# Later output weights, later keys, and global rows stored ahead of the last blocks: a fused attention and feed-forward kernel

## The chip, the cores and the metric

The kernel runs on one core of one Trainium2 chip. The metric is device time in microseconds (us), the median of several executions; shorter is better. PE is the matmul engine, DVE, ACT and POOL are the vector, scalar and GpSimd engines, and SP issues transfers. SP's and POOL's queues are strictly in order: a transfer waits until all that stands ahead of it on its queue has been issued.

## The reference

Sparse attention (a window of 32 positions to each side, plus 8 global positions that see and are seen by all), then a feed-forward layer with a sine activation:

```python
batch, n_heads, seq, head_dim = (8, 8, 576, 64)
scores = scale * np.matmul(q, k.transpose(0, 1, 3, 2))
mask = np.abs(pos[:, None] - pos[None, :]) <= window        # window = 32
mask = mask | is_global[:, None] | is_global[None, :]
scores = np.where(mask, scores, -1000000000.0)
...
attn = np.exp(scores); attn = attn / (np.sum(attn, axis=-1, keepdims=True) + 1e-09)
attn_out = np.matmul(attn, v)
x = attn_out.transpose(0, 2, 1, 3).reshape(B * S, H * D)    # 4608 x 512
h = x @ w_in                                                # 512 -> 2048
s = np.sin(alpha * h)
g = h + s * s / (alpha + 1e-09)
out = g @ w_out                                             # 2048 -> 512, float32
```

## The kernel before

The program is one straight list of instructions per engine, in the order in which the Python code issues them; no scheduler moves anything. It walks through the eight batches (b = 0 to 7). For each batch there is an attention and a GEMM 1 (x times w_in with the sine behind it, 16 groups of 128 columns, `gemm1`, loop over `nt`). The second product, `gemm2`, is a generator: it yields after each of its matmuls (128x512, L1172), and `fill(n)` takes n of them into PE's list wherever the code calls it. So GEMM 2 of batch b is spread over the attention and the GEMM 1 of batch b+1. How many are taken where is set by small tables: `FIRST`, `SECOND`, `NEAR`, `MIDST` in the attention (`LATE_FIRST`, `LATE_SECOND` in batch 1's), `PER_GROUP` in GEMM 1, `GROUP_LATE` in batch 1's, `GROUP_LAST` in the last one. A block of GEMM 2 is 128 rows; its 16 matmuls end in one PSUM bank (`zo`), ACT copies it to `osb` (L1182), and SP stores it (L1189). Even batches have four blocks, odd ones five.

An attention works on four head pairs (hp). For each it computes scores in two parts (PE, L929), the exponential on ACT (L938), the mask on DVE (L939), then `denominators` and, one to two pairs later, `numerators` (both PE, L967). `numerators` multiplies with V (tile VX or VD, in turn by batch) and DVE normalises with the reciprocal R into xT (L985). Batch 0 has an attention of its own.

K, Q and V come in steps. POOL casts them from DRAM to bf16 copies in DRAM (`cast_qk` L335, `cast_v` L342). SP loads V into SBUF (`load_v`, L418, four loads, the second half of them for the upper partitions) and transposes K and Q (`turn_qk`, L348) into the one pair of tiles kt and qt; DVE copies these into KX and QX (`place`, L364 and L357, eight copies per batch, the first four of them keys). `places_at` says in which attention, and behind which head pair, DVE makes which of the eight copies for the next batch. `pace(src)` is a one-element copy on POOL: as POOL's queue is in order, everything behind it waits until `src` has been written.

The weights are cast on the way from DRAM: w_in in four loads (L430), w_out in four (L436), each a quarter of the rows, 4 of the 16 `nt` steps of every block.

Global positions attend to all keys, so their rows are built from sums over all blocks (`global_sums`) and normalised at the very end. They run through the last GEMM 1 as 64 further columns (so 640 columns, not 576), and `gemm2_globals` (L1200) multiplies them with w_out and writes the 64 finished rows over the output with one indexed store on POOL (L1208), which must come after the stores of the same rows by `gemm2`. Last, `judge` tests whether the fast path's approximations hold; every engine loads the verdict (L1314) and branches (L1315) over a general path that is not run here.

The places around the change, with the counts that steer them:

```python
START = 1
FIRST, SECOND = (8, 6, 5, 5), (4, 4, 4, 4)
LATE_FIRST, LATE_SECOND = (0, 0, 3, 5), (0, 0, 3, 4)
NEAR, MIDST = 3, 6
PER_GROUP = (0, 0, 5) + 11 * (1,) + (0, 0)
```

Of the kernel before, what the change touches and what calls it, by code (L numbers as in the profile page):

```python
# [12 lines left out]
DT = mybir.dt  # L13
# [5 lines left out]
NG = 8  # L19
# [230 lines left out]
def kernel(  # L250
# [66 lines left out]
    seen = main.tile([1, 1], DT.bfloat16, name="seen")  # L317
# [21 lines left out]
    def cast_v(b):  # L339

        cast[b, "vd"] = dramp.tile([S, H, D], DT.bfloat16, name="vd")
        nc.gpsimd.dma_start(out=cast[b, "vd"][:], in_=v[b].rearrange("h s d -> s h d"))  # L342

# [553 lines left out]
    def attention(b, beside):  # L897
# [118 lines left out]
        inverse(last - 1)  # L1016
        numerators(last - 1)
        fill(NEAR)
# [87 lines left out]
    def gemm1(b):  # L1106
# [23 lines left out]
        for nt in range(NT):  # L1130
# [35 lines left out]

    def gemm2(b):
        lo, hi = (0, 4) if b % 2 == 0 else (4, 9)
        for blk in range(lo, hi):
            ops = zo[(blk + b // 2) % 2]  # L1170
            for nt in range(NT):
                nc.tensor.matmul(  # L1172
                    out=ops[:], lhsT=H2[:, nt, blk * P : (blk + 1) * P], rhs=w_out[:, nt, :],
                    start=(nt == 0), stop=(nt == NT - 1),
                )
                yield True
            osb = osbp.tile([P, DM], DT.float32, name="osb")
            if b == B - 1 and blk == hi - 1:
                for e, copy in enumerate((nc.scalar.copy, nc.vector.tensor_copy)):
                    copy(out=osb[:, e * DM // 2 : (e + 1) * DM // 2], in_=ops[:, e * DM // 2 : (e + 1) * DM // 2])  # L1180
            else:
                nc.scalar.copy(out=osb[:], in_=ops[:])  # L1182

            c = blk * P
            while c < (blk + 1) * P:
                z = min((c // QTR + 1) * QTR, (blk + 1) * P)
                run, u = c // QTR, c % QTR
                t0 = (b // 2) * 2 * S + (run // 2) * HALF + run % 2 + 2 * u
                nc.sync.dma_start(  # L1189
                    out=out[t0 : t0 + 2 * (z - c) - 1 : 2, :], in_=osb[c - blk * P : z - blk * P, :]  # L1190
                )
                c = z
# [46 lines left out]
    def pace(src):  # L1239

        nc.gpsimd.tensor_copy(out=seen[:], in_=src)  # L1241

    def phase_a(b_att, b_moe):
        def beside(at):

            if b_moe is None:
                if at == 0:
                    second_half()
                    turn_qk(1)
                    pace(turned[1][1][0:1, 0:1])  # L1250
                    load_w_in((2, 3))
                    cast_v(1)
                    load_w_out()
                    gather(v, gv)
# [28 lines left out]
    for b in range(B):  # L1283
        if b == 1:
# [30 lines left out]
    with tc.If(sure < P):  # L1315
# [31 lines left out]
```

## Time and profile before

| | us |
|---|---|
| median of 3 runs | 382.05 |
| lowest and highest run | 378.55, 384.41 |
| the profiled execution | 384.38 |
| its span, first to last instruction | 382.7 |
| PE busy | 323.6 (85%) |
| ACT busy | 288.9 (75%) |
| DVE busy | 275.5 (72%) |
| POOL busy | 55.1 (14%) |

Mean granted clock of PE: 0.97 of full speed. The profile has two kinds of rows that matter below. A timeline row gives the start in us from the span's start, the duration, the engine and source line, what it did (written tile <- read tiles) and how many instructions were merged into it; a bracket gives the engine's idle time just before and what ended it. A window row gives, for a stretch of time, its length, the busy time of PE, weight loads, DVE, ACT and POOL, the granted clock, the share of the 16 transfer engines (over 1 where transfers overlap) and the rate in GB/s. A busy PE is not PE at its peak, since matmuls overlap. "SPq" and "POOLq" are the queues' own instructions, the issue of transfers among them.

### The profile page before, as it was taken

The numbers are of one execution on the slowest core, as the hardware profiler recorded it, in microseconds if no ns is written. First come the engines' busy times: TensorE is split into PE (matmuls) and PEld (weight loads), VectorE is DVE, ScalarE is ACT, GpSimd is POOL, SyncE is SP. The second block draws the span as 40 slices with busy tenths as digits, with TensorE's granted clock in tenths as the row PEclk, the third lists the DMA queues.
The fourth block names the chain that finished last, engine by engine and source line by source line (L and its number), as shares of the span: only waits on it lengthen the run. The fifth ranks groups of instructions, "written<-read, shape, count | busy, mean of one in ns | idle before, by whom it ended". The sixth has DMA issues, their size and how long they took to land. (4 is left out here: it accounts for less than half of the span.)

```text
span 382.7 us, 10443 instructions
## 1 busy us (share of the span) xinstructions
PE 323.6 (85%) x4222; PEld 206.1 (54%) x4280; DVE 275.5 (72%) x539; ACT 288.9 (75%) x425; POOL 55.1 (14%) x78
## 2 busy tenths in 40 slices
PE   2678753699988998899899989998998998899990
PEld 2566532356645664566556655665466655554440
DVE  6966897156969687967796788778877885889400
ACT  7879794278877888879887987898888886889110
POOL 7941730014004000400030002100000000000001
PEclk9999995599999999999999999999999999999996
DMA  7999999179994991395849693977232020002221
GB/s 121 117 162 170 184 207 224 27 153 153 203 196 80 208 183 30 69 189 100 149 81 163 119 153 86 146 155 123 59 93 51 0 58 32 3 0 83 64 75 49
DMA packets 91393, 43.23 MB, mean 113 GB/s; under 512 B 76394, under 2 KB 85994, under 8 KB 90890
## 3 DMA queue, kind: packets, MB, share of 16 engines
q0 software_dynamic: 44208, 18.52, 39.9%
q1 hardware_dynamic: 47130, 23.97, 30.2%
q8 instruction: 35, 0.57, 0.6%
q14 instruction: 20, 0.16, 0.1%
HBM read 41.97 MB, written 21.95 MB: 167 GB/s over the span
## 5 line engine op out<-in xcount | busy, mean ns | idle before, releaser
L1172 PE MATMUL zo<-w_out,H 128*128 128x512 bf16 x518 | 137.5, 382 | 4.6 <-issue 3.6
L1124 PEld LDWEIGHTS <-w_in 128*128 128x128 bf16 x1024 | 99.2, 98 | 53.0 <-issue 18.7
L1172 PEld LDWEIGHTS <-H 128*128 128x128 bf16 x576 | 51.0, 98 | 45.3 <-issue 0.7
L938 ACT ACTIVATE E<-ring 128x720 bf16<-128x720 f32 x56 | 43.3, 773 | 28.8 <-PE ring L929 28.8
L1124 PE MATMUL zn<-xT,w_in 128*128 128x288 bf16 (+1 forms) x384 | 57.0, 287 | 6.1 <-DVE H L1160 4.1
L1124 PE MATMUL zr<-xT,w_in 128*128 128x288 bf16 x320 | 47.7, 287 | 3.3 <-DVE H L1160 2.9
L1124 PE MATMUL zd<-xT,w_in 128*128 128x288 bf16 x320 | 46.3, 287 | 1.9 <-DMA w_in<-in_moe_w_in_dram 1.3
L1160 DVE SCALAR_TENSOR_TENSOR H<-s,recipT,zn 128x576 bf16<-128x576 bf16 (+1 forms) x48 | 39.4, 822 | 10.7 <-ACT s L1157 7.3
L1154 ACT ACTIVATE sb<-zn,alphaT 128x576 bf16<-128x576 f32 (+1 forms) x48 | 35.7, 743 | 14.6 <-PE zn L1124 13.5
L1157 ACT ACTIVATE s<-sb 128x576 bf16<-128x576 bf16 (+1 forms) x62 | 42.7, 689 | 2.0
L1159 DVE TENSOR_TENSOR s<-sb 128x576 bf16<-128x576 bf16 (+1 forms) x66 | 30.9, 468 | 14.2 <-ACT sb L1154 13.1
L939 DVE TENSOR_TENSOR E<-E,MASKT 128x720 bf16<-128x720 bf16 x56 | 29.2, 529 | 11.6 <-ACT E L938 11.1
L1160 DVE SCALAR_TENSOR_TENSOR H<-s,recipT,zd 128x576 bf16<-128x576 bf16 (+1 forms) x40 | 32.9, 822 | 6.4 <-ACT s L1157 4.3
L1160 DVE SCALAR_TENSOR_TENSOR H<-s,recipT,zr 128x576 bf16<-128x576 bf16 (+1 forms) x40 | 32.9, 822 | 5.9 <-ACT s L1157 3.4
L1154 ACT ACTIVATE sb<-zd,alphaT 128x576 bf16<-128x576 f32 (+1 forms) x40 | 29.6, 739 | 5.9 <-PE zd L1124 5.9
L1154 ACT ACTIVATE sb<-zr,alphaT 128x576 bf16<-128x576 f32 (+1 forms) x40 | 29.6, 741 | 3.5 <-PE zr L1124 3.4
L1182 ACT COPY osb<-zo 128x512 f32<-128x512 f32 x35 | 20.4, 582 | 14.2 <-PE zo L1172 14.1
L778 ACT ACTIVATE R<-L,shift 128x576 f32<-128x576 f32 x32 | 24.8, 774 | 0.6
L985 DVE TENSOR_TENSOR xT<-zn,R 128x576 bf16<-128x576 f32 x21 | 15.8, 754 | 8.8 <-PE zn L967 6.0
L1241 POOL COPY seen<-xT 1x1 bf16<-1x1 bf16 x4 | 1.9, 480 | 134.7 <-DVE GN L755 134.7
L1208 POOL DMA_INDIRECT out_dram<-osb,grow x1 | 1.0, 979 | 135.7 <-SPq L1315 135.7
L929 PEld LDWEIGHTS <-KX 64*64 64x64 bf16 x448 | 9.0, 111 | 20.9 <-issue 19.2
(169 smaller groups left out, 373.5 us busy)
## 6 DMA issues: line engine op xcount, KB each, us to landing
kd<-in_k_dram POOLq DMA_DIRECT2D x7, 576.0 KB, 6.5
qd<-in_q_dram POOLq DMA_DIRECT2D x7, 576.0 KB, 10.1
vd<-in_v_dram POOLq DMA_DIRECT2D x7, 576.0 KB, 15.4
VX<-vd SPq DMA_DIRECT2D x16, 168.0 KB
w_in<-in_moe_w_in_dram POOLq DMA_DIRECT2D x4, 512.0 KB, 5.8
w_out<-in_moe_w_out_dram POOLq DMA_DIRECT2D x4, 512.0 KB, 16.4
out_dram<-osb SPq DMA_DIRECT2D x8, 256.0 KB
VD<-vd SPq DMA_DIRECT2D x12, 168.0 KB
```

Source lines behind the costliest of these rows:

```text
L778: nc.scalar.activation(out=R[:], in_=L[:], func=AF.Exp, scale=-1.0, bias=shift[:, 0:1])
L929: nc.tensor.matmul(out=zs[half * D : (half + 1) * D, t, 0 : G3 * WCOL].rearrange("p (m x c) -> p m x c", x=2, c=60)[:, m % G3, :, c0:c1], ...
L938: nc.scalar.activation(out=Eg, in_=zs[:, :, 0 : G3 * WCOL], func=AF.Exp, scale=scale)
L939: nc.vector.tensor_tensor(out=Eg, in0=Eg, in1=MASKT[:, None, G3 * g : G3 * (g + 1), :].rearrange("p o m c -> p o (m c)").to_broadcast([P, ...
L985: nc.vector.tensor_tensor(out=xT[:, hp, 0:S].rearrange("p (k m c) -> p k m c", k=4, c=KT), in0=tokens(nd(hp, 0)), in1=Rs[hp][:], op=ALU.mult,)
L1124: nc.tensor.matmul(out=h_part, lhsT=w_in[:, c, nt * P : (nt + 1) * P], rhs=xT[:, c, lo:hi], start=(c == 0), stop=(c == CT - 1), skip_group ...
L1154: nc.scalar.activation(out=sb[:, 0:W], in_=h, func=AF.Sin, scale=alphaT[:, nt : nt + 1])
L1157: nc.scalar.activation(out=s2[:, 0:W], in_=sb[:, 0:W], func=AF.Square)
L1159: nc.vector.tensor_tensor(out=s2[:, 0:W], in0=sb[:, 0:W], in1=sb[:, 0:W], op=ALU.mult)
L1160: nc.vector.scalar_tensor_tensor(out=H2[:, nt, r0 : r0 + W], in0=s2[:, 0:W], scalar=recipT[:, nt : nt + 1], in1=h, op0=ALU.mult, op1=ALU.add,)
L1172: nc.tensor.matmul(out=ops[:], lhsT=H2[:, nt, blk * P : (blk + 1) * P], rhs=w_out[:, nt, :], start=(nt == 0), stop=(nt == NT - 1),)
L1182: nc.scalar.copy(out=osb[:], in_=ops[:])
```

## The change

Five things change.

1. `load_w_out` moves from batch 0's attention to batch 0's GEMM 1 (nt = 10), behind the copies of the global keys and queries, and a `pace` on one column of VX[1]'s upper half stands ahead of it. On POOL's queue it is now ahead of the casts of batch 2's K and Q.
2. For batch 3, `places_at` gives the first two key copies behind head pair 2 and the other six behind the attention, where it gave 2, 1, 3 and 2 at four places.
3. In every attention but batch 0's, `fill(NEAR)` stands ahead of `numerators(last - 1)` and not behind it.
4. The global rows are multiplied and stored ahead of the last batch's five blocks. So that these blocks do not write other values over batch 7's global rows, POOL first copies batch 7's eight global columns of H2 onto their token columns (`put_globals`). The columns' numbers are worked out on DVE and loaded into POOL registers ahead of batch 2's GEMM 1 (`load_columns`). `GROUP_LAST` takes 16 matmuls of GEMM 2 into the last GEMM 1 instead of 4, and the rest of batch 6's stands ahead of the global rows.
5. The last block is computed in two halves of 256 columns, in two PSUM banks, each evicted by ACT and stored by itself (`store`). The closing branch has its preferred side changed.

```diff
@@ numerators and fill
         inverse(last - 1)
+        fill(NEAR)
         numerators(last - 1)
-        fill(NEAR)
         denominators(last)
@@ gemm1, b == 0 and nt == 10
                 load_vg(1)
+                pace(VX[1][D : D + KT, 0, 0, 0:1])
+                load_w_out()
@@
+    def load_columns():
+        ...
+        nc.vector.tensor_copy(out=ci[:, 0], in_=gi32[:, 0::2])
+        ...
+        nc.vector.tensor_scalar(out=gcol[:], in0=cf[:, 3], scalar1=float(S), scalar2=None, op0=ALU.add)
+        for j in range(NG):
+            columns_of.append(nc.gpsimd.value_load(gcol[0:1, j : j + 1], min_val=S, max_val=2 * S - 1))
+
+    def put_globals():
+        for j, c in enumerate(columns_of):
+            g = 2 * S + j * B + B - 1
+            nc.gpsimd.tensor_copy(out=H2[:, :, bass.ds(c, 1)], in_=H2[:, :, g : g + 1])
@@ gemm2
+            parts = 2 if (b, blk) == (B - 1, hi - 1) else 1
+            for part in range(parts):
+                cols = slice(part * DM // parts, (part + 1) * DM // parts)
+                if part:
+                    ops = zd[:, 1]
+                for nt in range(NT):
+                    nc.tensor.matmul(
+                        out=ops[:, cols], lhsT=H2[:, nt, blk * P : (blk + 1) * P], rhs=w_out[:, nt, cols],
+                        start=(nt == 0), stop=(nt == NT - 1), skip_group_check=True,
+                    )
+                    yield True
+                nc.scalar.copy(out=osb[:, cols], in_=ops[:, cols])
+                store(b, blk, osb, cols)
@@
-    GROUP_LAST = (0, 0, 2) + 2 * (0, 0, 0, 1) + 5 * (0,)
+    GROUP_LAST = (0, 0, 3) + 13 * (1,)
@@ places_at
-        share = {-1: (0, 2), 1: (2, 3), 2: (3, 6), 4: (6, 8)}
+        share = {2: (0, 2), 4: (2, 8)} if b_att == 2 else {-1: (0, 2), 1: (2, 3), 2: (3, 6), 4: (6, 8)}
@@ phase_a, batch 0
                     cast_v(1)
-                    load_w_out()
                     gather(v, gv)
@@ main loop and tail
     for b in range(B):
+        if b == 2:
+            load_columns()
...
-    waiting.append(gemm2(B - 1))
+    put_globals()
     square_x(B - 1, 0)
     square_x(B - 1, 1)
-    for c in range(CT):
+    square_w(0)
+    fill(NT)
+    square_w(1)
+    fill(4 * NT)
+    gemm2_globals()
+    judge_sums()
+    waiting.append(gemm2(B - 1))
+    for c in (2, 3):
         square_w(c)
         fill(NT)
-        if c == 1:
-            judge_sums()
     judge()
     fill(2 * NT * NT)
-    gemm2_globals()
...
-    with tc.If(sure < P):
+    with tc.If(sure < P, preferred_fallthrough_block=False):
```

How the instructions move is seen in each engine's list. First POOL's, from w_in's second half to the copy that releases batch 2's V (`vd`, `kd`, `qd` are the DRAM copies, `seen` the target of `pace`). Before:

```order
L430 DMA w_in<-in_moe_w_in_dram 128x4x512 x2
L342 DMA vd<-in_v_dram 4608x1x64
L436 DMA w_out<-in_moe_w_out_dram 128x4x512 x4
L1260 COPY MASKT<-MASK 64x720 x2
L719 CAST VGb<-H_97 64x512
L377 COPY KX_94<-kTg 128x48x8
L380 COPY QX_96<-qTg 128x4x7x4 x2
L335 DMA kd<-in_k_dram 32x9216
L335 DMA qd<-in_q_dram 32x9216
L1241 COPY seen<-qt 1x1
```

And in the changed kernel:

```order
L435 DMA w_in<-in_moe_w_in_dram 128x4x512 x2
L343 DMA vd<-in_v_dram 4608x1x64
L1294 COPY MASKT<-MASK 64x720 x2
L724 CAST VGb<-H_97 64x512
L382 COPY KX_94<-kTg 128x48x8
L385 COPY QX_96<-qTg 128x4x7x4 x2
L347 COPY seen<-VX_93 48x1
L441 DMA w_out<-in_moe_w_out_dram 128x4x512 x4
L336 DMA kd<-in_k_dram 32x9216
L336 DMA qd<-in_q_dram 32x9216
L347 COPY seen<-qt 1x1
```

The four loads of w_out have moved behind the four other POOL copies and a copy that reads VX, and stand directly ahead of batch 2's K and Q.

Next DVE's list at the end of batch 2's attention, from the last global sums to the first group of GEMM 1 (`kt`, `qt` are batch 3's transposed keys and queries). Before:

```order
L755 TENSOR_REDUCE GN<-zd 128x2x4
L357 COPY QX_96<-qt 64x4x6x48 x2
L1159 TENSOR_TENSOR s_2256<-sb 128x576
L1160 SCALAR_TENSOR_TENSOR H_97<-s_2256,recipT,zn 128x576
L1160 SCALAR_TENSOR_TENSOR H_97<-s_2263,recipT,zr 128x576
```

And in the changed kernel:

```order
L760 TENSOR_REDUCE GN<-zd 128x2x4
L369 COPY KX_94<-kt 64x48x24 x2
L362 COPY QX_96<-qt 64x4x6x48 x4
L1180 COPY ci<-girow 1x8
L1181 TENSOR_SCALAR ci<-ci 1x8
L1182 CAST cf<-ci 1x16
L1183 TENSOR_SCALAR cf<-cf 1x8
L1186 SCALAR_TENSOR_TENSOR cf<-cf 1x8
L1189 SCALAR_TENSOR_TENSOR cf<-cf 1x8
L1192 TENSOR_SCALAR gcol<-cf 1x8
L1166 TENSOR_TENSOR s_2340<-sb 128x576
L1167 SCALAR_TENSOR_TENSOR H_97<-s_2340,recipT,zn 128x576
```

Four more copies and seven one-row instructions now stand between the attention and the first group's square; the two key copies that stood ahead of the attention's first masks are gone from there.

Last, SP's list at the end of the program (the stores of the last blocks, the verdict and the branch). Before:

```order
L1314 TENSOR_LOAD verdict
L1314 ISA x2
L1189 DMA out_dram<-osb 80x512
L1189 DMA out_dram<-osb 48x512
L1189 DMA out_dram<-osb 96x512
L1189 DMA out_dram<-osb 32x512
L1189 DMA out_dram<-osb 112x512
L1189 DMA out_dram<-osb 16x512
L1189 DMA out_dram<-osb 128x512
L1315 COMPARE_AND_BRANCH
```

And in the changed kernel:

```order
L1228 DMA out_dram<-osb 96x512
L1228 DMA out_dram<-osb 32x512
L1354 TENSOR_LOAD verdict
L1354 ISA x2
L1228 DMA out_dram<-osb 112x512
L1228 DMA out_dram<-osb 16x512
L1228 DMA out_dram<-osb 128x256 x2
L1355 COMPARE_AND_BRANCH
L1355 UNCONDITIONAL_BRANCH
```

The verdict is loaded two blocks later, the last block's store has become two, and an unconditional jump follows the compare. POOL's indexed store is no longer behind these stores: the first store of the last batch waits for it. PE's list has, behind the last GEMM 1, 39 matmuls of batch 6's GEMM 2 where 50 stood, then the 32 of the global rows, then batch 7's blocks.

More of the change, by code (lines that the diff above doesn't have):

```diff
@@ L316 @@
     VG0 = main.tile([NG * B, D], DT.bfloat16, name="VG0")
-    seen = main.tile([1, 1], DT.bfloat16, name="seen")
+    seen = main.tile([P, 1], DT.bfloat16, name="seen")
+    gcol = main.tile([1, NG], DT.int32, name="gcol")
     girow = main.tile([1, NG], DT.int64, name="girow")
@@ L342, in cast_v, with pace @@
         nc.gpsimd.dma_start(out=cast[b, "vd"][:], in_=v[b].rearrange("h s d -> s h d"))
+    def pace(src):
+        nc.gpsimd.tensor_copy(out=seen[0 : src.shape[0]], in_=src)
     def turn_qk(b):
```

46 lines of the change are left out of this document (24 added, 22 removed).

## The prediction

> **What bounds the kernel now.** I read the page first (busy shares, slices, granted clock), then the waits of PE, then the timeline stage by stage. The page's last three slices rows say where to look: the granted clock is full except around 57 to 77 us, and the transfer engines stand still in the slice that follows their fullest one.
>
> ```profile
> PEclk9999995599999999999999999999999999999996
> DMA  7999999179994991395849693977232020002221
> ```
>
> From batch 2 on PE is the bound: matmuls follow each other with gaps of tenths. Three places are not so: attention 1, attention 2 and the end. The largest is the first, where PE waits twice for V; these are PE's rows (start, duration, what; in brackets the idle time before and its end):
>
> ```profile
> 67.89 0.28 PE L967 MATMUL zn<-E,VX 56*64 56x88 bf16 x2 [4.82 <-DMA VX<-VGb]
> 70.56 0.78 PE L967 MATMUL zn<-E,VX 56*64 56x88 bf16 x26 [2.39 <-DMA VX<-VGb]
> ...
> 78.01 0.82 PE L1172 MATMUL zo<-w_out,H 128*128 128x512 bf16 x3
> ```
>
> 4.82 + 2.39 = 7.2 us are lost there, and the work could have started at 67.89 - 4.82 = 63.1. Why V is late is seen in POOL's and SP's own queues: w_out is issued right behind batch 1's V cast, V's four loads into SBUF leave SP only when that cast has landed, and then w_out and the next batch's K and Q (52.22) are on the same engines.
>
> ```profile
> 38.41 2.26 POOL L342 DMA_DIRECT2D vd<-in_v_dram  x1
> 40.12 3.53 POOL L436 DMA_DIRECT2D w_out<-in_moe_w_out_dram  x4
> ...
> 52.22 0.53 POOL L335 DMA_DIRECT2D kd<-in_k_dram  x1
> ...
> 83.97 0.18 POOL L1241 COPY seen<-qt 1x1 bf16<-1x1 bf16 x1 [30.65 <-DMA qt<-qd]
> ```
> ```profile
> 51.60 1.63 SPq L418 DMA_DIRECT2D VX<-vd  x4
> ...
> 75.18 2.21 SPq L348 DMA_TRANSPOSE kt<-kd  x1
> ...
> 93.61 1.60 SPq L418 DMA_DIRECT2D VD<-vd  x4
> ```
>
> **V and w_out (term A).** w_out leaves the queue ahead of batch 1's loads and comes back behind a copy that waits for V's second half. V's cast landed by 51.60, and this is kept: w_out stood behind it in the same queue. What V's loads take on engines that do nothing else is shown by batch 7, whose loads are issued at 282.59; the columns that matter are the last two, DMA share and GB/s:
>
> ```profile
> 282.59 1.68 SPq L418 DMA_DIRECT2D VX<-vd  x4
> ```
> ```profile
> 52.00:54.00 2.00, 1.22 (x10) 0.68 (x7) 1.89 (x5) 1.92 (x3) 1.32 (x3) 1.00 1.24 208
> 62.00:64.00 2.00, 0.69 (x14) 0.33 (x14) 1.95 (x6) 0.87 (x2) 0.00 (x0) 0.50 1.28 273
> 288.00:290.00 2.00, 2.00 (x17) 1.53 (x16) 1.33 (x2) 1.97 (x3) 0.00 (x0) 1.00 0.28 45
> 290.00:292.00 2.00, 1.76 (x13) 1.11 (x12) 1.31 (x3) 1.97 (x4) 0.00 (x0) 1.00 0.00 0
> ```
>
> All is moved by 290.0, 7.4 us after the first issue, against 70.56 - 51.60 = 19.0 in batch 1. So V lands at the latest at 51.60 + 7.4 = 59.0, ahead of 63.1: the V wait goes. What is late next is w_out, the first thing PE needs behind V.
>
> ```profile
> w_in<-in_moe_w_in_dram POOLq DMA_DIRECT2D x4, 512.0 KB, 5.8
> w_out<-in_moe_w_out_dram POOLq DMA_DIRECT2D x4, 512.0 KB, 16.4
> ```
>
> The nearest row for an undisturbed 512 KB load is w_in's, 5.8 us. With half a microsecond for the copy, the first quarter lands at 59.0 + 0.5 + 5.8 = 65.3, each further one 524 KB at 208 GB/s = 2.5 us later (the window from 52, when mostly w_out moved): the fourth at 72.9. PE takes w_out in fills of 3, 3, 5 and 4 matmuls; the thirteenth, the first that needs the fourth quarter, is the second of the fill at 78.01, so at 78.2, or at 71.0 with 7.2 us gone. It would stand 1.9 us there: A = -5.3. If V's second half, which is what the copy waits for, lands 2 us ahead of the last of the six loads, nothing is waited for: A = -7.2. I take **-6.0**; with w_out's row of 16.4 it would be far less (a rival). PE's half clock (0.50 in the window from 62) moves along with the stage.
>
> Behind w_out on POOL stand batch 2's K and Q. They land about 73 + 2 x 2.5 = 78, but today SP comes to their transposes only at 75.18, held by the late attention. So the copy of qt that releases the next casts stays near 83.97, and V of batch 2 near 93.61 + 7.4 = 101. Its reader comes at 115.11, or 109: this hides it.
>
> ```profile
> 115.11 0.48 PE L967 MATMUL zn<-E,VD 56*64 56x88 bf16 x28
> ```
>
> **Batch 3's keys (term B).** DVE stands 3.29 us for their transpose, ahead of the masks of attention 2. The table loads mark the stages: attention 2 lasts 126.05 - 107.00 = 19.05, attention 4, without such a wait, 204.51 - 187.17 = 17.34. The change gains the 1.7 between.
>
> ```profile
> 107.00 1.28 ACT L905 ACT_TABLE_LOAD   x1
> 126.05 1.28 ACT L1021 ACT_TABLE_LOAD   x1
> 187.17 1.28 ACT L905 ACT_TABLE_LOAD   x1
> 204.51 1.28 ACT L1021 ACT_TABLE_LOAD   x1
> ```
> ```profile
> 111.68 0.92 DVE L364 COPY KX<-kt 64x1152 bf16<-64x1152 bf16 x2 [3.29 <-DMA kt<-kd]
> ...
> 127.42 0.93 DVE L357 COPY QX<-qt 64x1152 bf16<-64x1152 bf16 x2
> 128.97 0.46 DVE L1159 TENSOR_TENSOR s<-sb 128x576 bf16<-128x576 bf16 x1 [0.62 <-ACT sb L1154]
> ...
> 359.11 0.15 DVE L1095 TENSOR_SCALAR oks<-cm 128x1 f32<-128x1 f32 x1
> ```
>
> But behind the last normalisation DVE now does six copies instead of two (4 x 0.46 = 1.8) and seven one-row instructions for the column numbers (at 0.15, 1.1), with the first square of GEMM 1 queued behind them: 2.9 us, less the 0.62 that DVE idles there now, is 2.3. PE gets its fourth group's PSUM that much later; I take 2.0, since a little of PE's idle time there is used. B = **+0.3**, from -1.7 (pile hidden) to +2.3 (no gain in the attention). The eight register loads on POOL wait for this too; only the cast for batch 5, which waits for a later attention anyway, is behind them.
>
> **Three fills ahead of the numerators (term C).** In seven attentions PE now goes from one run of fills to the products and no longer turns to 128-row weights between numerators and the last denominators. Such a turn costs what PE idles at it:
>
> ```profile
> 201.94 0.59 PE L1172 MATMUL zo<-w_out,H 128*128 128x512 bf16 x2 [0.16 <-issue]
> ```
>
> 7 x 0.16 = **-1.1**; a second turn saved would double it to -2.2. The numerators now end three fills later, 3 x 0.22 = 0.66, and DVE's normalisation reads them; but it waits for the reciprocal from ACT there, 2.6 us in six attentions:
>
> ```profile
> DVE xT L985 <- ACT R L778: 2.6, 6, 0.9
> ```
>
> So 0.43 of each 0.66 is covered, and the rest would be 7 x 0.23 = +1.6, if anything waited for it: that is the upper end.
>
> **The last GEMM 1 and the tail (term D).** The order has 39 matmuls of batch 6's GEMM 2 behind the last GEMM 1, where 50 stood: 11 move in.
>
> ```profile
> 326.82 1.25 PE L1124 MATMUL zn<-xT,w_in 128*128 128x288 bf16 x8 [0.60 <-DVE H L1160]
> 327.90 1.25 PE L1124 MATMUL zr<-xT,w_in 128*128 128x288 bf16 x8
> ...
> 332.02 1.25 PE L1124 MATMUL zr<-xT,w_in 128*128 128x288 bf16 x8
> ...
> 342.12 1.25 PE L1124 MATMUL zn<-xT,w_in 128*128 128x288 bf16 x8
> 343.21 13.98 PE L1172 MATMUL zo<-w_out,H 128*128 128x512 bf16 x62
> ```
>
> One matmul is 13.98 / 64 = 0.22 (two records are missing). Out of the tail go 11 x 0.22 = 2.4. A group is 1.08 of PE (326.82 to 327.90) but comes every (342.12 - 332.02) / 8 = 1.26, so 0.18 of each fill is free and 0.04 is not: 0.5 in all if all of it fits, 2.4 if none does; I take 0.9. The last block in halves has 32 matmuls of 256 columns; at the group's pace, 1.08 / 8 = 0.135 for about 320, each takes some 0.12 with its weights, 3.8 instead of 16 x 0.22 = 3.5. D = -2.4 + 0.9 + 0.4 = **-1.1**, from -2.0 to +0.4. The eight column copies on POOL lie beside the 39 fills and the global rows (39 x 0.22 + 1.9 = 10.5 us).
>
> **The end (term E).** Behind PE's last matmul, 372.06 + 1.94 = 374.0, come 8.7 us today: evictions, the last store's landing at 375.7 (issued 373.07), then the scatter, its landing near 381, and the closing barriers, 1.7.
>
> ```profile
> 372.06 1.94 PE L1200 MATMUL zd<-w_out,H 128*64 128x256 bf16 x32
> ```
> ```profile
> L1208 POOLq EVENT_SEMAPHORE  x5: 17/43/43, 368.3 to 375.7; - x5
> ```
> ```profile
> L1342 SPq EVENT_SEMAPHORE  x14: 17/28/28, 381.0 to 382.6; - x14
> ```
> ```profile
> L1315 PEldq COMPARE_BRANCH  x1: 4318/4318/4318, 373.2 to 373.2; - x1
> ```
>
> With the scatter ahead of the last stores the end is one half's eviction (0.5), a landing (2.6) and 1.7: 4.9. The scatter itself is hidden by five blocks of 3.5 us. But PE's branch, 4.3 us from 0.8 before its last matmul's end, was covered by the scatter and is so no longer: 3.5 + 0.1 + 1.7 = 5.3. The branch's preferred side changes, which may or may not remove that; I take 5.3, so E = **-3.4**, at best -3.8. [...]
>
> **Rivals.** *w_out comes as slowly as now.* Its row of 16.4 from the fourth issue at 59.5 + 2.2 gives 78.1, as late as it is used today: A = 0, and the rest, -5.3, remains: 376.8. For it: K and Q of batch 2 still follow it. Against: 208 GB/s needs no 16 us.
>
> *The two transfers in a row, slower than before.* They are now side by side. If each keeps its duration, V lands at 67.89 and the fourth quarter at 68.4 + 2.2 + 16.4 = 87.0, against 78.2 in use: A = +8.8, total +3.5: 385.6. This mechanism decides from a landing of 78.2 + 5.3 = 83.5 on. Against it stands the engines' full share beside V (1.28 from 62), so that they do slow each other.
>
> [...]
>
> **How the numbers follow.** -6.0 + 0.3 - 1.1 - 1.1 - 3.4 = -11.3. The profiled execution took 384.38 (span 382.7, and 1.7 around it) and would take 373.1; it lies 2.3 above the median of 382.05, whose own runs spread over 5.9, so the forecast is 382.05 - 11.3 = **370.8**, its own range 366 to 375. Chances: forecast 0.62, slow w_out 0.18, late copies 0.12, transfers in a row 0.04, anything worse 0.04. A range of 366 to 378 takes in the first three but for their outer ends. A change of 2%, 7.6 us, is about what a measurement of this kernel tells: faster means under 374.4. Nine tenths of the forecast and half of the late copies lie there, and a little of slow w_out: 0.63. Slower (over 389.7): 0.05. The rest, 0.32, is no change.
>
> **What would show it.** In the changed profile: no wait for V in batch 1's attention, w_out's loads landing in 6 to 9 us and a PE wait of 0 to 2 us at L1214 ahead of the fourth fill; attention 2 near 17.3 us with GEMM 1 of batch 2 some 2 us longer; PE's fills each about 0.22 between the last groups; the scatter landed while blocks are still computed, and 5 us from the last matmul to the end. It is wrong if w_out's median landing stays at 16, if the casts behind qt move later than 84, or if PE waits for POOL at the tail.

## The result, and the profile after

The changed kernel takes 377.26 us (18 runs, 374.88 to 379.64), the kernel before 381.1 (18 runs, 378.27 to 387.73). The ratio is 0.991, with a 95% interval of 0.988 to 0.994: shorter by 0.9%, which is clear of the noise but under the 2% that the prediction set for a change, and not the 3% forecast. Ratios, here and below, are against executions of the kernel before on the same chip, and leave out those more than 1.5% above the fastest of their kernel. The profiled execution of after has a span of 377.93, against 382.68; both are longer executions than their medians, so the 4.75 us between them is not quite the 3.84 between the medians.

The table loads mark the stages, as in the prediction (ACT loads one table at the start of each attention and one at the start of each GEMM 1). With PE's last matmul they divide the 4.75 us between the two spans:

| stage | before | after | difference |
|---|---|---|---|
| up to attention 1 | 54.87 | 55.67 | +0.80 |
| attention 1 | 27.33 | 22.22 | -5.11 |
| GEMM 1 of batch 1 | 24.80 | 24.80 | 0 |
| attention 2 | 19.05 | 20.80 | +1.75 |
| GEMM 1 of batch 2 | 21.72 | 24.25 | +2.53 |
| attention 3 to attention 7 | 173.24 | 172.15 | -1.09 |
| last GEMM 1 up to the last matmul | 52.98 | 51.53 | -1.45 |
| from there to the end | 8.69 | 6.51 | -2.18 |

The first two rows belong together. Over all profiles of this document attention 1 starts anywhere from 54.9 to 58.7, but ends at 77.3 to 78.4 where w_out's move is in and at 81.5 to 83.2 where it is not: the move's gain up to there is -5.11 + 0.80 = -4.3 here.

In attention 1 the waits went nearly as forecast. PE's rows there, and POOL's that set them:

```profile
65.06 0.58 PE L1214 MATMUL zo<-w_out,H 128*128 128x512 bf16 x1 [0.15 <-DMA w_out<-in_moe_w_out_dram]
...
68.66 0.59 PE L1214 MATMUL zo<-w_out,H 128*128 128x512 bf16 x2 [0.60 <-DMA w_out<-in_moe_w_out_dram]
...
71.20 0.81 PE L1214 MATMUL zo<-w_out,H 128*128 128x512 bf16 x3 [0.82 <-DMA w_out<-in_moe_w_out_dram]
...
73.77 1.46 PE L1214 MATMUL zo<-w_out,H 128*128 128x512 bf16 x5 [0.83 <-DMA w_out<-in_moe_w_out_dram]
```
```profile
58.56 0.19 POOL L347 COPY seen<-VX 48x1 bf16<-48x1 bf16 x1 [5.90 <-DMA VX<-vd]
59.02 3.01 POOL L441 DMA_DIRECT2D w_out<-in_moe_w_out_dram  x4 [0.27 <-issue]
...
84.97 0.18 POOL L347 COPY seen<-qt 1x1 bf16<-1x1 bf16 x1 [21.75 <-DMA qt<-qd]
```

V is there at 58.5, no matmul waits for it, and the four waits for w_out come to 2.4 us. But the last row is where it was: the copy that releases the next casts stood at 83.97 before and stands at 84.97 now. By the start of attention 3 (147.77 before, 147.74 after) the whole gain is gone. These are ACT's marks of attention 2, GEMM 1 of batch 2 and attention 3, and PE's rows in between:

```profile
102.69 1.28 ACT L910 ACT_TABLE_LOAD   x1
123.49 1.28 ACT L1026 ACT_TABLE_LOAD   x1
147.74 1.28 ACT L910 ACT_TABLE_LOAD   x1
```
```profile
111.29 0.28 PE L972 MATMUL zd<-E,ones 56*64 56x88 bf16 x8
114.26 0.41 PE L972 MATMUL zd<-E,ones 56*64 56x120 bf16 x20 [2.69 <-issue]
114.60 1.04 PE L1214 MATMUL zo<-w_out,H 128*128 128x512 bf16 x4
...
116.94 1.91 PE L1214 MATMUL zo<-w_out,H 128*128 128x512 bf16 x4 [0.34 <-issue]
...
130.37 1.14 PE L1129 MATMUL zn<-xT,w_in 128*128 128x288 bf16 x8 [2.47 <-DVE H L1167]
```

There are two holes. In the first PE stops in the middle of a set of 28 denominator matmuls, behind the eighth, and waits for nothing that the profile shows. Soon after, four matmuls of a fill take 1.91 us instead of 1.04. The windows (columns as in the prediction) show why: the granted clock, the third column from the end, falls to a half.

```profile
112.00:114.00 2.00, 0.00 (x0) 0.00 (x0) 1.07 (x3) 0.29 (x1) 1.37 (x3) 1.00 1.15 77
114.00:116.00 2.00, 1.74 (x49) 1.05 (x52) 0.59 (x2) 0.65 (x1) 1.86 (x2) 0.92 1.47 315
116.00:118.00 2.00, 1.67 (x34) 1.06 (x26) 1.96 (x4) 1.82 (x3) 0.43 (x1) 0.50 1.03 194
```

The second hole, 2.47 us, is the pile on DVE ahead of the first groups of GEMM 1:

```profile
124.87 0.93 DVE L369 COPY KX<-kt 64x1152 bf16<-64x1152 bf16 x2
125.82 1.86 DVE L362 COPY QX<-qt 64x1152 bf16<-64x1152 bf16 x4
127.72 0.16 DVE L1180 COPY ci<-girow 1x8 int32<-1x8 int32 x1
...
128.95 0.44 DVE L1166 TENSOR_TENSOR s<-sb 128x576 bf16<-128x576 bf16 x1
```

At the end, the last matmul is over at 369.51 + 1.91 = 371.42. PE's branch, now a compare and a jump, is in the second block (its two parts, shortest, median and longest in ns, and their starts):

```profile
369.51 1.91 PE L1214 MATMUL zd<-w_out,H 128*128 128x256 bf16 x16
```
```profile
L1355 PEldq COMPARE_BRANCH  x2: 91/2030/3970, 370.3 to 371.6; - x2
```

### The profile page after: what moved, and what is told of

Same layout as the page of the kernel before. It is cut to its first block, busy times and chain, and to the rows that moved or that the text cites. A ratio compares the mean times of both kernels' runs of the same rounds, so it can differ in the third digit from the quotient of the medians.

```text
span 377.9 us, 10527 instructions
## 1 busy us (share of the span) xinstructions
PE 323.3 (86%) x4238; PEld 208.2 (55%) x4296; DVE 277.5 (73%) x545; ACT 288.7 (76%) x426; POOL 59.6 (16%) x87
## 4 chain that ended last, share of the span: by engine, by line
PE 45%; DMA 15%; DVE 14%; ACT 13%; issue 6%; POOL 5%; SPq 0%; DVEq 0%; ACTq 0%; POOLq 0%
PE zo L1214 22%; PE zn L1129 8%; ACT sb L1161 6%; DVE H L1167 5%; PE zr L1129 4%; DMA kt<-kd 4%; PE zd L1129 4%; DMA vd<-in_v_dram 3%; DMA w_out<-in_moe_w_out_dram 3%; PE ring L934 2%; DVE s L1166 2%; DMA kd<-in_k_dram 2%; PE zn L972 2%; DMA VD<-in_v_dram 2%; PE zd L972 2%
## 5 line engine op out<-in xcount | busy, mean ns | idle before, releaser
L1214 PE MATMUL zo<-w_out,H 128*128 128x512 bf16 (+1 forms) x518 | 137.5, 380 | 7.2 <-issue 3.9
L1214 PEld LDWEIGHTS <-H 128*128 128x128 bf16 x592 | 53.2, 98 | 47.8 <-issue 4.6
L1219 ACT COPY osb<-zo 128x512 f32<-128x512 f32 (+1 forms) x36 | 20.7, 574 | 13.9 <-PE zo L1214 7.7
L1201 POOL COPY H<-H 128x16 bf16 x8 | 5.0, 629 | 105.4 <-DVE H L1167 104.9
```

Source lines behind the costliest of these rows:

```text
L1214: nc.tensor.matmul(out=ops[:, cols], lhsT=H2[:, nt, blk * P : (blk + 1) * P], rhs=w_out[:, nt, cols], start=(nt == 0), stop=(nt == NT - 1) ...
L1219: nc.scalar.copy(out=osb[:, cols], in_=ops[:, cols])
```

## The experiments

The first question was what ate the gain of attention 1. One theory (K) said that batch 3's keys come at a fixed time; a rival (S) that PE's stall and the pile are troubles of their own.

**w_out's move alone**, in the kernel before:

```diff
                 load_vg(1)
+                pace(VX[1][D : D + KT, 0, 0, 0:1])
+                load_w_out()
...
                     cast_v(1)
-                    load_w_out()
```

> The kernel before with w_out's move alone. Theory K (the keys of batch 3 land at a fixed time, because their cast waits for batch 2's queries, so that an earlier attention 2 only waits longer for them): attention 1 lasts 22.2 us as in the changed kernel instead of 27.3, and DVE's wait for kt in attention 2 grows from 3.3 to 7 or 8 us, attention 2 from 19.05 to 23 or 24. The time is 0 to 1 us below the kernel before. Rival S (the keys move along with the earlier work, and what the changed kernel lost in attention 2 came from PE's stall there and from the pile of copies): the wait for kt stays at 3 us, attention 2 at 19, and the time is 4 to 5 us below the kernel before.

387.72 us, *longer* than the kernel before: ratio 1.019 (1.012 to 1.027). Attention 1 lasts 22.20, as in the changed kernel, but attention 2 27.94 instead of 19.05. DVE's and PE's rows, and two windows:

```profile
113.18 0.92 DVE L368 COPY KX<-kt 64x1152 bf16<-64x1152 bf16 x2 [9.16 <-DMA kt<-kd]
```
```profile
114.72 0.96 PE L971 MATMUL zd<-E,ones 56*64 56x88 bf16 x28 [6.68 <-DVE E L943]
```
```profile
112.00:113.00 1.00, 0.00 (x0) 0.00 (x0) 0.00 (x0) 0.00 (x0) 0.00 (x0) 0.50 0.20 38
...
118.00:119.00 1.00, 1.00 (x30) 0.67 (x21) 0.93 (x3) 1.00 (x2) 0.00 (x0) 0.50 0.00 0
```

K holds in that the keys do not come earlier, and both theories missed a second loss. The keys land at 113.18 (111.68 before), though attention 2 starts 4.4 us earlier; DVE waits 9.16 for them instead of 3.29, and in and behind that wait PE runs at half clock, from 111 to 121.

**The late keys undone**, the rest of the change kept:

```diff
-        share = {2: (0, 2), 4: (2, 8)} if b_att == 2 else {-1: (0, 2), 1: (2, 3), 2: (3, 6), 4: (6, 8)}
+        share = {-1: (0, 2), 1: (2, 3), 2: (3, 6), 4: (6, 8)}
```

> The changed kernel with batch 3's copies at their four old places. Theory K: DVE waits 7 to 8 us for kt at the start of attention 2, attention 2 lasts 23 to 24 us (20.8 in the changed kernel), GEMM 1 of batch 2, with the seven one-row instructions but without the four more copies, 22.8 (24.25): together 46 to 47 against 45.05, and the time is 0 to 2 us above the changed kernel. Rival S: attention 2 19 and GEMM 1 22.8, together 41.8, and the time 3 us below the changed kernel: the late placing is then a loss.

382.09 us, 4.8 above the changed kernel, ratio to before 1.004 (1.000 to 1.009). Attention 2 takes 27.32 (DVE waits 10.26 for kt, PE 7.78, half clock again), GEMM 1 of batch 2 22.37. So without the late placing nothing is left of w_out's gain, and the seven one-row instructions alone cost 0.65 of GEMM 1.

**The clock's share.** w_out's move alone again, with 28 further matmuls of 128x512, whose result is not used, where PE waits for the keys:

```diff
+            if b == 2 and hp == 1:
+                warm(zd[:, 0], 28)
             if hp:
                 denominators(hp - 1)
```

> The kernel before with w_out's move alone, and 28 further matmuls of 128x512 (6.1 us at full clock; their result is not used) where PE waits 6.7 us for batch 3's keys in attention 2. It computes the same besides. Theory H (of the 8.9 us that attention 2 lost there, 4.4 are the longer wait for the keys, and the other 4 to 5 are PE's half clock from 111 to 121, which follows the idle time): the granted clock stays at 1.00 through attention 2, which falls from 27.9 to 23.0 to 24.0, and the time is 4 to 5 us below w_out's move alone, about that of the kernel before. Rival (the clock does not matter, since DVE and the transfers bound that stage): attention 2 stays at 27 to 28.

```profile
112.00:114.00 2.00, 2.00 (x11) 0.91 (x10) 0.00 (x0) 0.00 (x0) 0.00 (x0) 1.00 1.14 73
```

The clock stays at 1.00 throughout, attention 2 falls from 27.94 to 25.59, and the time from 387.72 (386.30 to 389.21) to 385.31 (382.60 to 387.34). So the half clock is some 2.4 of the 8.9 us, not the 4 to 5 expected; the rest is the wait. DVE's copy comes 11.2 us after the start of attention 2 (114.23 - 103.01), where it was 4.7 before the change: 6.5 later, not 4.4, and 19.05 + 6.5 = 25.6. (In w_out's move alone the copy came 10.55 after the start; by the same sum its wait explains 5.9 and the half clock 3.0.) The keys did not only stand still. SP issues their transpose at 103.44 before and 103.43 with w_out's move alone, but they land 1.5 us later; why was not tested.

**No pile, no copies in attention 2.** The changed kernel with batch 3's copies one by one in the groups of GEMM 1, and the column numbers in attention 1:

```diff
+            if b == 2 and 4 <= nt < 12:
+                which, t, y = PLACES[nt - 4]
+                place(b + 1, which, t, y, nc.vector.tensor_copy)
...
+            if b_att == 1 and at == 2:
+                load_columns()
```

> The changed kernel without the pile: batch 3's eight copies go one by one into groups 4 to 11 of GEMM 1 of batch 2 (group 11's square moves from DVE to ACT), and the column numbers are worked out in attention 1, where DVE idles. If the pile is what GEMM 1 of batch 2 lost: it falls from 24.25 to 21.7 to 22.5 us, and attention 2, without any copy, from 20.8 to 17.3 if PE's stall of 2.7 us does not recur, or to 19 to 20 if it does. The time is 2 to 5 us below the changed kernel. Rival (GEMM 1 of batch 2 is held by something else, or DVE has no room for eight copies between its groups): GEMM 1 of batch 2 stays above 23.5 and the time within 1 us of the changed kernel.

377.23 us, as the changed kernel: the rival was right. Attention 2 is 20.31 with the same stall (2.43 us, again behind the eighth of 28 matmuls, at full clock after it, and a second one of 1.15), and GEMM 1 of batch 2 is 23.89: PE waits about half a microsecond for DVE at one group after another. DVE has no room for eight copies there, whether in a pile or apart.

**Earlier casts.** The copy that holds back the casts of batch 2's V and batch 3's K and Q reads kt instead of qt:

```diff
-            pace(turned[2][0][0:1, 0:1])
+            pace(turned[2][1][0:1, 0:1])
```

> The changed kernel with one edit: the copy that holds back the casts of batch 2's V and batch 3's K and Q reads kt, which is written first, and not qt. The casts are issued at 81 to 82 us instead of 86.3, so batch 3's transposes leave SP at about 99 to 100 instead of 103.3. Theory F (PE's stall of 2.7 us in attention 2 is a load of its instructions that runs while qt's transposes are moved, and the half clock follows from it): qt has been moved by 112, the stall shrinks below 1 us, the clock stays full, and attention 2 falls from 20.8 to 17.3 to 18.5; the time is 2 to 4 us below the changed kernel. Rival (the stall belongs to the place in PE's list, or casts and transposes beside each other slow one another by as much): a stall of 2 us and more stays, and the time is within 1 us of the changed kernel.

374.95 us, ratio to before 0.988 (0.978 to 0.998), 2.3 below the changed kernel; the interval takes in the changed kernel's 0.991, so that the stages have to tell. The casts came only 1.7 us earlier (from 84.53, not 86.26) and the keys' transpose 1.3 (102.04, not 103.31). That was enough for attention 2, which is 17.22. PE's rows there and at the pile, and a window behind the pile:

```profile
112.45 0.41 PE L972 MATMUL zd<-E,ones 56*64 56x120 bf16 x20 [0.68 <-issue]
...
127.00 1.59 PE L1129 MATMUL zn<-xT,w_in 128*128 128x288 bf16 x8 [2.46 <-DVE H L1167]
```
```profile
128.00:130.00 2.00, 2.00 (x9) 1.12 (x8) 0.86 (x2) 1.34 (x3) 0.00 (x0) 0.50 1.07 163
```

The stall shrank with the transposes, as theory F said. The pile is now the first long stop of PE, and this time the half clock follows *it*: GEMM 1 of batch 2 is 25.33 instead of 24.25.

What PE waits for in the stall is seen only in the trace's transfer records, where the engines' own instructions come in as 16 KB transfers (queue q8, 35 of them in the changed kernel). The table sets the first of these after attention 2's start beside SP's issue of the queries' transpose (which stands behind the keys'):

| kernel | attention 2 starts | queries' transpose issued by | load starts | PE stands |
|---|---|---|---|---|
| earlier casts, spread copies, old w_out (below) | 107.31 | 108.22 | 111.96 | 0 |
| before | 107.00 | 111.62 | 113.05 | 0 |
| changed | 102.69 | 113.77 | 111.63 | 2.69, to 114.26 |
| changed, copies in GEMM 1 | 102.29 | 113.28 | 111.13 | 2.43, to 113.59 |
| earlier casts | 102.91 | 111.94 | 109.80 | 0.68, to 112.45 |
| earlier casts, spread copies | 102.12 | 110.98 | 108.84 | 0.36, to 111.36 |

SP is done with the queries' transpose when the keys have landed, within 0.1 us (111.62 and 111.68 in the kernel before). Where the transposes are long issued, the load starts 4.65 us after attention 2, when PE has begun some 2,000 of its instructions. Where they are not, it starts 2.11 to 2.16 us before SP is done with the second one, in all eleven profiles of that kind (at PE's instruction 2,231 in the changed kernel), and where PE stands it goes on 2.4 to 2.65 us after the load's start. It comes to that spot 8.9 us after attention 2's start in each of them. So the load waits among the keys' transposes, and PE can stand for it. That the stall follows the transposes was tested; that the transfer is PE's is read from a count: 33 of these transfers start ahead of the last matmul, one for some 260 of PE's 8,583 instructions, and no other engine has more than 738.

**The pile undone as well.** On top of the earlier casts, three copies behind head pair 2, three behind head pair 3 and two at the end of attention 2, and the column numbers in attention 1:

```diff
-        share = {2: (0, 2), 4: (2, 8)} if b_att == 2 else {-1: (0, 2), 1: (2, 3), 2: (3, 6), 4: (6, 8)}
+        share = {2: (0, 3), 3: (3, 6), 4: (6, 8)} if b_att == 2 else {-1: (0, 2), 1: (2, 3), 2: (3, 6), 4: (6, 8)}
```

> The edit of the run before, and batch 3's eight copies spread over attention 2 (three behind head pair 2, three behind head pair 3, two at the end), and the column numbers worked out in attention 1. Theory (GEMM 1 of batch 2 is longer by what DVE has to do at its head: 1.9 us for four more copies, 0.6 for the one-row instructions): GEMM 1 of batch 2 goes back from 24.25 to 21.7 to 22.3, attention 2 is 0.5 to 1 us longer than without the spread, together 1 to 2 us less than with the earlier casts alone and 3 to 6 us below the changed kernel. Rival (DVE's work is the bound of attention 2 and GEMM 1 together, wherever the copies stand, as eight copies inside GEMM 1 made it 23.9): the two together do not get shorter.

```profile
102.12 1.28 ACT L910 ACT_TABLE_LOAD   x1
119.03 1.28 ACT L1026 ACT_TABLE_LOAD   x1
140.76 1.28 ACT L910 ACT_TABLE_LOAD   x1
```

372.31 us, ratio 0.983 (0.976 to 0.989). Attention 2 is 16.91 and GEMM 1 of batch 2 21.73: both losses are gone, and the copies cost nothing there. Together the two stages are 2.4 us shorter than even the prediction expected of the change itself (17.3 and 2 us more than 21.72).

**The end.** The kernel before with parts 4 and 5 alone, which is the changed kernel without parts 1 to 3 (w_out and the key copies as in the two edits at their old places, and the fills):

```diff
         inverse(last - 1)
-        fill(NEAR)
         numerators(last - 1)
+        fill(NEAR)
```

> The kernel before with the global rows, the column copies, the halves and the branch alone (parts 4 and 5). From the two traces: 1.4 us less between the last GEMM 1 and the last matmul, 2.2 less behind it, and up to 1.1 more at the head of GEMM 1 of batch 2 for the seven one-row instructions: 2.5 to 3.6 us below the kernel before. By the terms of the prediction (1.1 and 3.4) it would be 4.5. Rival (the end moves with each run, and the traces only happened to differ): within 1 us of the kernel before, with 8 us or more from the last matmul to the end.

379.92 us, against 381.84 for the kernel before beside it (four executions between 373.86 and 381.65, too far apart for a verdict). The stages are clear: 51.54 up to the last matmul and 6.66 behind it, as in the changed kernel (51.53 and 6.51), against 52.98 and 8.69; GEMM 1 of batch 2, with the one-row instructions, is 22.34, 0.6 longer. The differences at the end belong to these parts. Next, the changed kernel with the old branch:

```diff
-    with tc.If(sure < P, preferred_fallthrough_block=False):
+    with tc.If(sure < P):
```

> The changed kernel with the closing branch as before, everything else kept. If the preferred side bought nothing, as the prediction took it: the same 6.5 us from the last matmul to the end, with PE's branch at 4.0 to 4.3 us. If it is worth something: up to 1 us more here. Rival: the branch without the jump behind it falls through without a stall, PE's branch is under 0.2 us, and the end comes no earlier than the last store's landing allows, about 5.5 to 6.5 us.

```profile
L1355 PEldq COMPARE_BRANCH  x1: 3742/3742/3742, 371.7 to 371.7; - x1
```

None of the three expectations held. There is still a stall, 3.74 us, but the end comes 4.71 us after the last matmul instead of 6.51. The single branch starts at 371.7, 1.1 *before* the last matmul's end at 372.77. In the changed kernel the compare is quick (91 ns), and the jump behind it stalls for 3.97 from 371.62, 0.2 *after* the last matmul's end at 371.42. But it is not PE that the end waits for. These are SP's waits for its stores to land (L1355), and SP's and PE's arrivals at the closing barrier (L1382), first in the changed kernel and then in this run:

```profile
L1355 SPq EVENT_SEMAPHORE  x8: 17/17/17, 372.4 to 375.3; - x8
L1382 SPq DRAIN  x3: 7/7/13, 376.7 to 377.3; - x3
L1382 PEldq DRAIN  x2: 8/40/73, 375.6 to 377.4; - x2
```
```profile
L1355 SPq EVENT_SEMAPHORE  x8: 17/17/17, 374.1 to 375.1; - x8
L1382 SPq DRAIN  x3: 7/7/13, 375.9 to 376.4; - x3
L1382 PEldq DRAIN  x2: 8/8/8, 375.6 to 376.5; - x2
```

In the changed kernel PE is at the barrier at 375.6, and SP, behind the last landing at 375.3 and a jump of its own, at 376.7.

In both kernels SP issues the last store 0.4 us after the last matmul, but it lands 3.9 us after the matmul with the jump and 2.3 without. The transfer records show the difference. With the jump, a 16 KB instruction load runs from 1.1 to 2.7 us after the last matmul, beside the store, and 9 of the store's 144 packets end only behind it, at 2.8 to 3.4. Without the jump the load is over at 1.1, and all packets have ended by 1.8. So it is in all seven profiles that have the jump (landing at 3.7 to 4.1) and in the five that have the old branch and the halves (2.2 to 2.8). The new preferred side costs 1.8 us; that it does so mainly by a load in the store's way is read from these records and was not tested by itself.

The whole time, 376.28 (374.00 to 379.27), is 1.0 below the changed kernel's, but its ratio to the kernel before, 0.991, is the same, so the time by itself proves nothing.

**Earlier casts, spread copies and the old branch together**, the three edits shown:

> The earlier casts, the spread copies and the early column numbers, with the closing branch as before the change (no jump behind the compare). From the two runs that did the one and the other: 1.6 to 1.8 us from the last matmul to the end less than with the jump (4.7 for 6.35), attention 2 and GEMM 1 of batch 2 at 16.9 and 21.7 us, 370 to 371 us in all, 10 to 12 below the kernel before. Rival (the jump's 1.8 us was a difference between two runs): the end stays at 6.3 to 6.7 and the time at 372 to 373.

370.72 us, ratio 0.974 (0.970 to 0.979), with 4.89 us behind the last matmul: the fastest version, 6.5 us below the changed kernel. And with the last block whole:

```diff
-            parts = 2 if (b, blk) == (B - 1, hi - 1) else 1
+            parts = 1
```

> The same kernel with the last block computed and stored whole. By the prediction's terms its 16 matmuls take 3.5 us and 32 halves 3.8, and a whole eviction 0.6 and a half 0.4: the last matmul comes 0.2 to 0.4 us earlier and the time behind it is 0.2 to 0.3 longer where the store's landing bounds the end, and not longer where PE's branch does. So the time stays within 0.5 us. Rival (the halves are what shortens the end): 1 us and more longer behind the last matmul.

371.70 us, and 5.79 behind the last matmul: a microsecond longer, so the rival's reading holds for the end. PE's branch is over before the last matmul ends here; what is later is the last store's landing, 3.6 us after the last matmul where it was 2.2. The halves themselves cost nothing ahead of it (51.58 with the whole block, 51.53 without), not the 0.4 of the prediction. (Attention 2 happened to start 0.9 earlier in this profile, at 102.09, and was 1.5 longer, 18.37: PE stood 1.46 us in the same stall, until 112.42. With the transposes where they are, coming earlier is no gain.)

**What is w_out's move worth?** In the changed kernel:

```diff
                 load_vg(1)
-                pace(VX[1][D : D + KT, 0, 0, 0:1])
-                load_w_out()
...
                     cast_v(1)
+                    load_w_out()
```

> The changed kernel with w_out loaded at its old place, everything else kept. Theory (the move of w_out saved 5 us in attention 1 and lost most of it again in attention 2, since PE came too early for its own instructions): attention 1 lasts 26 to 27.5 us (22.2 in the changed kernel), attention 2, with the late key copies and no stall, 17.0 to 17.6 (20.8), GEMM 1 of batch 2 still 24 (the pile stays): 1 to 2 us above the changed kernel. Rival (the move is worth its 5 us): 5 us above it, at 382. Other rival (V's wait is short in most executions and only the profiled one showed it long): at or below the changed kernel.

The load at its old place gives 379.01 us (377.95 to 380.31), 1.7 above the changed kernel; but the kernel before was slower beside these runs too (385.16), and the ratio, 0.985 (0.981 to 0.989), is no worse than the changed kernel's 0.991. In the profile, attention 1 is 25.42, attention 2 16.35 without any stall, GEMM 1 of batch 2 25.20 with the half clock behind the pile: 66.97 together, against 22.22 + 20.80 + 24.25 = 67.27. The move gains 3.2 in the first stage and gives it back in the other two together. In the kernel with the earlier casts, the spread copies and the old branch, the same edit:

> The kernel of the run before, with w_out loaded where the kernel before loads it. If the move of w_out is worth its whole 5 to 6 us as soon as the keys of batch 3 are no longer waited for: attention 1 lasts 27 us instead of 21.4, attention 2 and GEMM 1 of batch 2 stay at 17 and 21.7, and the time is 4.5 to 6 us above the run before. Rival (something behind attention 1 is set by transfers and takes the gain back here too): the time is within 2 us of it.

372.94 us, but between 367.91 and 376.07: no answer. Both were therefore timed again, side by side:

> The kernel with the earlier casts, the spread copies and the old branch, with w_out at its old place, in more executions than before, since four of them lay between 367.9 and 376.1. If the move of w_out is worth 4 to 5 us there: a median 4 to 5 above the same kernel with the move, 374.5 to 375.5. If V's wait varies from one execution to the next and is short in about half of them: a median 0 to 2.5 above it, with a spread of 8 us against 2.4.

> The same kernel with w_out's move, on the same chip as its counterpart: 370 to 371.5, with a spread of 2 to 3 us.

374.19 us (373.03 to 375.47) without the move, 371.02 (369.94 to 372.14) with it: 3.2 us, ratios to before 0.972 and 0.964. The spread expected of the former, 8 us, did not come; V's wait was long again:

```profile
70.45 1.11 PE L972 MATMUL zn<-E,VX 56*64 56x88 bf16 x28 [6.60 <-DMA VX<-VGb]
```

So the move is worth 3.2 us once attention 2 can take it, close to nothing in the kernel as changed (by the ratios it may even cost a little), and costs 6 alone. The two executions near 368 to 370 of the first attempt stay unexplained.

## Why the prediction was wrong, by its own steps

| term | predicted | in the traces |
|---|---|---|
| V and w_out (A) | -6.0 | -5.1, in attention 1 |
| batch 3's keys (B) | +0.3 | +4.3 |
| fills ahead of the numerators (C) | -1.1 | -1.1, in attentions 3 to 7 |
| last GEMM 1 and tail (D) | -1.1 | -1.45 |
| the end (E) | -3.4 | -2.2 |
| start of the program | 0 | +0.8 |
| sum | -11.3 | -4.75 |

**A's mechanism was right in itself, and failed at what comes behind it.** V landed by 58.5 (59.0 was the bound), w_out took 9.8 us at the median (6 to 9 were said), PE waited 2.4 (0 to 2). The computed -5.3 was closer than the -6.0 chosen, and -4.3 is what is left at the end of attention 1. The step that failed is "So the copy of qt that releases the next casts stays near 83.97 ... this hides it". The first half came nearly true (84.97, where the prediction had named later than 84 as a sign of being wrong) and should have been the alarm: attention 2 came 4.3 us earlier (102.69, not 107.00), and behind that copy stand not only batch 2's V, whose reader I looked up, but batch 3's keys as well, and their transposes. I priced the keys in B from the kernel before, where attention 2 starts at 107, and added the two terms. They do not add: A without the late placing is +6 in the runs, A with it about 0.

**B.** "The change gains the 1.7 between": without w_out's move attention 2 gains more, 2.7 (19.05 to 16.35, some 0.4 of it from C, as in the attentions behind it). With it, the stall of 2.69 and the half clock behind it stand in its place, and attention 2 is 1.75 longer. Of the pile "I take 2.0": PE's hole was 2.47 and GEMM 1 grew by 2.53, and by 3.5 to 3.6 where the half clock followed. The order of DVE's list had been read rightly; the clock had no term. Whether it follows a stop is partly luck, as the last section shows.

**C and D have the right sum, C by luck.** The -1.1 of C is the sum over attentions 3 to 7: the 3rd, 5th and 6th are 0.4 shorter each, the 7th 0.2, and the 4th 0.35 longer, for a reason that stays open (over the profiles with the moved fills it lasts 17.0 to 17.7, with the old ones 17.3 to 18.1). So where the fills gain, they gain more than the 0.16 per attention of the prediction, nearer to the doubled figure that it named; some 0.4 more stands in B's row. In D the 0.4 for the halves was not there; without it the prediction's terms give -1.5, and -1.45 was measured. The column copies on POOL took 5.46 us, 0.68 each, and lay beside the fills, and PE waited for none of them; no run shows a hold-up that would bear out the 0.12 given to late copies. The slow w_out and the transfers in a row did not come either.

**E named the wrong last wait, at "PE's branch, 4.3 us from 0.8 before its last matmul's end".** The stall's length was about right (3.97), but the jump stalls after the last matmul and not before it. Even so PE is not the last at the closing barrier. The end goes by the path that the prediction gave for its best case, with other sizes: 0.4 to the last store's issue, 3.4 for its landing (2.6 had been taken) and 2.6 behind it (1.7 had been taken), together 6.5. With the old branch it is 0.4 + 1.9 + 2.4 = 4.7, so that the best case of 4.9 comes out with sizes that make up for each other. That PE's stall would stay was an estimate from the 4.32 us of the kernel before. It held: the stall is 3.97 and 3.79 on the jump (the changed kernel; earlier casts and spread copies) and 3.74 and 3.56 on the single compare (the old branch; the same with these casts and copies). I did not see that an instruction load would run beside the last store, from 1.1 to 2.7 us behind the last matmul.

None of the rivals' mechanisms was at work. The time came out where the slow w_out would have put it (376.8), for another reason.

## What to carry to other kernels

When a stage is pulled forward, list everything further on that keeps its own time (transfers behind a pacing copy, the transposes behind these, the engines' own instruction loads), not only the next reader; a term priced at the old start of the stage cannot be added to the gain. A stop of PE of some 2.5 us at the head of GEMM 1 of batch 2 cost another microsecond in the clock (3.5 to 3.6 us in all) or nothing (2.53), by where it lay in the clock's steps. The end came 6.51 us after the last matmul where the closing branch's stall began behind that matmul and an instruction load ran beside the last store, and 4.71 where the stall began 1.1 us ahead of that matmul's end: in a kernel like this one the branch is best placed so that both come under the last matmuls.

## What the runs showed of the hardware

- With transposes in flight a load of instructions (PE's, by the count above) came up to 4.3 us later here (8.9 instead of 4.65 us after attention 2's start), and PE stood up to 2.69 us for it. In the five profiles in which the load came with the transposes done or nearly so, PE did not stand for it.
- The granted clock changed in steps: in the kernel before and the changed kernel all stretches at half clock, but for the one at the program's end, last 3.41 us or a whole multiple of it (17.07; 10.24 and 3.41), and so do the stretches at full clock that follow them (300.37; 47.79 and 256.00). In attention 2 and GEMM 1 of batch 2 it fell to a half behind stops of 2.20, 2.46 and 2.69 us, for 3.41 us each, and did not fall behind stops of 1.46, 2.43 and 2.47. Where a fall shows how the steps lie, 2.0 us of the stop of 2.69, 2.1 to 2.5 of the stops of 2.46 and the whole one of 2.20 lay inside the step ahead of the fall, while the stop of 2.47, which no fall followed, was cut into 1.43 and 1.04. How the stop of 2.43 lay is not shown, nor a bound that holds elsewhere: in attention 1 of the changed kernel the clock, at a half already, stayed there from 64.48 to 67.89 behind a step in which PE stopped for 0.94 and 0.38 us. Behind 6.7 us of waiting, in w_out's move alone, the half clock lasted 10.2 us, to 6.4 us after PE had work again.
- From its issue to its landing the keys' transpose took 5.8 to 8.5 us in the five profiles in which PE's load came with the landing or after it, and 8.5 to 10.6 in the eleven in which the load fell in between. Whether the load or the other traffic of the earlier stage made it longer is not shown.
